# A gated delta-rule scan with a routed expert layer: late slot counts, the first expert's early scatters and later gathers placed elsewhere in a hand-written order

## The chip, the cores and the metric

The kernel runs on one core of one Trainium2 chip. The metric is device microseconds from launch to end, lower is better. A core has engines that run side by side, each through its own queue in program order: PE (matrix products), DVE (elementwise work and reductions), ACT (copies and activation functions), POOL (a general engine, which also issues indirect DMAs) and SP (which here only issues DMAs). A result passes between engines through semaphores, so an instruction that waits holds back everything behind it on its own queue.

## The reference

Two stages. The first is a recurrent attention with a state matrix for each of 4 batches and 8 heads; the second sends every token to one of 8 experts.

```python
B, H, S, D = 4, 8, 768, 48            # attention
N, DM, E, F = 3072, 384, 8, 1024      # experts; N = B * S, DM = H * D
k_n = k / (norm(k) + 1e-6)
for t in range(S):
    y[t] = q[t] @ state
    state = state + beta[t] * outer(k_n[t], v[t] - k_n[t] @ state)
x = y.reshape(N, DM)
logits = x @ w_gate
e = argmax(logits, 1)                 # one expert for each token
out[n] = softmax(logits)[n, e] * (relu(x[n] @ w1[e]) @ w2[e])
```

## The kernel before

**Attention.** The 768 steps are cut into 24 chunks of 32 (`NN = 24`), and the loop `for t in range(NN)` (line 882) runs over them. Inside one chunk the recurrence is solved by small matrix products over all 32 batch-head pairs at once. PE's order in a chunk is written out by hand: `residual` (line 369, product of keys and state into the PSUM bank `kb`, then DVE subtracts it from `v`, line 371), `state_out` (into `yb`), `apply` (line 376, into `kb`, which ACT copies to `u`, line 383), `turn` (line 419, transposes of the row before), `update` (line 385, into the state `S`, which ACT copies to `st` in two halves, line 396), `inside` (line 398, into `yb`), `logits` (line 449, for the chunk before, into `kb`; ACT copies it to `rl`, line 458). The bank `kb` is shared by `residual`, `apply`, `logits` and the counts described below, in different columns.

**Positions.** Between these steps stand seven calls `beside(t, i)` (line 869). Each sets a position `at[0] = 7*t + i` and hands out other work at that place of the order: DVE work from a list of generators up to a budget (`BUD`, 1.4 at i = 0, 1.3, 1.3, 1.3, 0.9, and nothing at i = 5 and 6), then, from chunk 20 on, `count_now()`, then steps of the weight pipeline `W` at the places in `WSL`, then steps of the first expert's early work at the places in `ES`.

**Routing.** `emit_slots` (line 473) is the generator that turns the logits of one to four chunks into a slot in the expert's list: maximum, one-hot `ohb` (lines 488 to 503, DVE); then a `count` on PE (lines 510 to 514, two or more small products into `kb`: how many tokens before this one chose the same expert), copied to `pc` by ACT (line 517); then the position in the list, `sli` (lines 525 to 551, DVE); then a write of the row to DRAM (`xn`, line 554, on SP) and a scatter of the token's number to `st_d` (line 555, on POOL). The count is put on a list `pend`, and `count_now` (line 464) issues everything that is on it. A generator asks for its next part only some positions after the part before (`lag`, 4 for the chunks up to 19, 2 for later ones). After the last chunk a loop (line 942) goes on giving out these steps, one position each, with one step of the early expert work in each of its rounds.

**Weights.** `pieces` (line 586) loads the weights of all experts in pieces of 128 rows (`w1`, 3 pieces of 512 KB) or 256 rows (`w2`, 4 pieces of 384 KB), in the order of experts, through three raw buffers (`load`, line 594, on SP). Each piece is split (line 582) into a rounded part `hi` and the remainder `lo`, so that a product is made of three. For the pieces 0 to 6, those of expert 0, DVE makes both parts; for later ones ACT makes `hi` and DVE `lo`. A piece's split is followed at once by the load of the piece three further on, which needs the same raw buffer. In chunks 20 to 23 the two first loads stand at (20, 3) and (20, 6), and the seven splits at (21, 1), (21, 3), (21, 5), (22, 1), (22, 3), (22, 5), (23, 1).

**Expert 0, early.** When the list of expert 0 has its first 256 tokens (chunks 0 to 15), they are gathered and computed ahead of the expert phase. `early` (line 690) does it in steps: `x` (transposes and splits, 3 steps), `h` (8 steps), `y` (2 steps, each ends with a scatter of 128 rows of the output, line 714). `rest` (line 717) prepares the remaining tokens of expert 0 in two steps, `t` and `o`. `EO` (line 95) is their order: `xxxhhhhhhhhytyo`.

**Expert phase.** For each expert, twelve steps t = 0 to 11 (line 1079): eight of the first product (`h`), then four groups of the second (`y`), each with a scatter of the output. Beside them, `tokens` (line 967) prepares the next expert: at t = 0 `fetch` gathers its rows by four indirect DMAs on POOL (line 632, into one of two buffers `XR`) and `find` loads the list of the one after it; at t = 6 the gate weights; at 8, 9 and 10 the transposes. `run(W)` at the steps in `PC` advances the weights of the next expert.

Of the kernel before, what the change touches and what calls it, by code (L numbers as in the profile page):

```python
# [8 lines left out]
F32 = mybir.dt.float32  # L9
# [4 lines left out]
ALU = mybir.AluOpType  # L14
# [6 lines left out]
NN = S // C  # L21
# [4 lines left out]
DM = H * D  # L26
E = 8
# [6 lines left out]
NG = 3  # L34
GW = [128] * NG + [CAP - 128 * NG]
ROW = DM + E + 2
# [5 lines left out]
def deltanet_moe(ctx, tc, kq, kn_in, v_in, bl_in, w_gate, w1, w2, out):  # L42
    nc = tc.nc
# [31 lines left out]
    W1 = 4  # L75
# [3 lines left out]
    AH = 3  # L79
# [3 lines left out]
    VA = 6  # L83
    RB = {4: 2, 1: 3}
    PL = (1, 3, 5)
    BUD = (1.4, 1.3, 1.3, 1.3, 0.9, 0.0, 0.0)
    TS = 5
    TOK = (0, 6, 8, 9, 10)
# [1 line left out]
    TOK0 = (0, 6, 8, 9, 10)  # L90
    PC0 = (0, 2, 5, 7, 8, 10, 11)
    WSL = ((20, 3), (20, 6), (21, 1), (21, 3), (21, 5), (22, 1), (22, 3), (22, 5), (23, 1))
    ES = ((23, 1), (23, 3), (23, 4), (23, 6))
    EF = tuple(range(0, 16))
    EO = 'xxxhhhhhhhhytyo'
# [2 lines left out]
    rp = ctx.enter_context(tc.tile_pool(name="rp", bufs=1, side="left"))  # L98
# [138 lines left out]
    at = [-1000]  # L237
# [91 lines left out]
    def lane_ops(tb):  # L329
        T = tiles[tb]  # L330
        lg, lw = T["lg"], T["lw"]
        G = nc.gpsimd if tb in PL else nc.vector
        for c in range(31):
# [128 lines left out]
    pend, order_ = [], []  # L462

    def count_now(more=lambda: None):
        now = list(pend)
        for x in now:
            x[0]()
        more()
        for x in now:
            x[1]()  # L470
            pend.remove(x)

    def emit_slots(n0, w, row, rl):
# [43 lines left out]
            nc.scalar.copy(out=pc, in_=pp)  # L517
            when.append(at[0])

        pend.append((count, keep))  # L520
        yield 0.2
        while not when or order_[0] != n0:
            yield None
# [45 lines left out]
    def run(gen, steps=1):  # L569

        for _ in range(steps):
            if next(gen, tiles) is tiles:
                return False
        return True
# [4 lines left out]

    KD, KF = DM // 128, FF // 128  # L580

    def split(hi, lo, src, copy=nc.scalar.copy):
        copy(out=hi, in_=src)  # L583
        nc.vector.tensor_tensor(out=lo, in0=src, in1=hi.bitcast(F32), op=ALU.subtract)  # L584

    def pieces():

        todo = []
        for e in range(E):
            for nm, src, kk, ff, st in (("w1", w1[e], KD, FF, 1), ("w2", w2[e], KF, DM, 2)):  # L590
                todo += [(e, nm, src.rearrange("(k p) f -> p k f", p=128), kk, ff, st, j) for j in range(0, kk, st)]
        raws = []

        def load(k):
            e, nm, sv, kk, ff, st, j = todo[k]
            raw = wq[0].tile([128, FF], F32, name=f"{nm}r{e}_{j}", tag="wr", bufs=3)
            if 0 < k < AH:
                nc.scalar.copy(out=raw[0:1, 0:1], in_=ident[0:1, 0:1])
            raws.append(raw[:, 0:st * ff].rearrange("p (k f) -> p k f", k=st))
            nc.sync.dma_start(out=raws[k], in_=sv[:, j:j + st])  # L600

        for k in range(AH):
            load(k)
            yield
        for k, (e, nm, sv, kk, ff, st, j) in enumerate(todo):
            if j == 0:
                WW[e][nm] = [wq[e % 2].tile([128, kk, ff], F32R, name=f"{nm}{x}{e}", tag=f"{nm}{x}") for x in "hl"]
            hi, lo = WW[e][nm]
            split(hi[:, j:j + st], lo[:, j:j + st], raws[k], nc.vector.tensor_copy if k < 7 else nc.scalar.copy)
            if k + AH < len(todo):  # L610
                load(k + AH)
            yield

    WW = [{} for _ in range(E)]

# [16 lines left out]
    def fetch(e, g0=0, g1=NG + 1, nt=NN):  # L632
        for g in range(g0, g1):
            nc.gpsimd.indirect_dma_start(out=XR[e][:, g], out_offset=None, in_=xn[0:128 * nt],  # L634
                                         in_offset=bass.IndirectOffsetOnAxis(ap=XI[e][:, g, 0:1], axis=0),
                                         bounds_check=128 * nt - 1, oob_is_err=False)

    def smalls(e, g0, g1, pool):

        n = g1 - g0  # L640
        ex = pool.tile([128, n, E], F32, name=f"ex{e}_{g0}", tag=f"ex{n}", bufs=2)
        gt = pool.tile([128, n], F32, name=f"gt{e}_{g0}", tag=f"gt{n}", bufs=2)
        x = XR[e][:, g0:g1]
        nc.scalar.activation(out=ex, in_=x[:, :, DM:DM + E], func=AF.Exp)
        nc.vector.tensor_reduce(out=gt, in_=ex, axis=AX.X, op=ALU.add)
        nc.vector.tensor_scalar(out=gt, in0=gt, scalar1=1e-9, scalar2=None, op0=ALU.add)
        nc.vector.reciprocal(gt, gt)
        return gt, XI[e][:, g0:g1, 1:2]
# [37 lines left out]
    def scatter(yo, idx):  # L686
        nc.gpsimd.indirect_dma_start(out=out, out_offset=bass.IndirectOffsetOnAxis(ap=idx, axis=0), in_=yo,  # L687
                                     in_offset=None, bounds_check=N - 1, oob_is_err=False)

    def early():  # L690

        w = 128 * G0
        xe = er_[0].tile([128, 2 * KD, w], F32R, name="xe")
        x = [xe[:, i * KD:i * KD + KD] for i in range(2)]
        for d in range(KD):
            pt = psg_[-1].tile([128, w], F32, name=f"xt{d}", tag="g")
            for g in range(G0):
                nc.tensor.transpose(pt[:, g * 128:g * 128 + 128], XR[0][:, g, d * 128:(d + 1) * 128], ident)
            split(x[0][:, d], x[1][:, d], pt)
            yield  # L700
        he = er_[0].tile([128, KF, 2, w], F32R, name="he")
        hs = [(he[:, f, 0], he[:, f, 1]) for f in range(KF)]
        for f in range(KF):
            ps = psg_[-1].tile([128, w], F32, name=f"h0_{f}", tag="g")
            first(ps, WW[0]["w1"], x, slice(f * 128, f * 128 + 128))
            relu(*hs[f], ps)
            yield
        gt, idx = smalls(0, 0, G0, er_[0])
        for g in range(G0):
            ps = psg_[-1].tile([128, DM], F32, name=f"y0_{g}", tag="g")  # L710
            second(ps, lambda f: [h[:, g * 128:g * 128 + 128] for h in hs[f]], WW[0]["w2"])
            yo = er_[0].tile([128, DM], F32, name=f"yo0_{g}")
            nc.scalar.activation(out=yo, in_=ps, func=AF.Copy, scale=gt[:, g:g + 1])
            scatter(yo, idx[:, g])
            yield

    def rest():
# [20 lines left out]
    er_ = []  # L738
# [70 lines left out]
    W = None  # L809
# [55 lines left out]
    def ahead_step():  # L865
        if order and not (order[0] == "o" and len(last) < DEF):
            run(other if order.pop(0) in "to" else ahead)

    def beside(t, i):
# [5 lines left out]
        if t >= NN - 4:  # L875
            count_now()
        for _ in range(WSL.count((t, i))):
            run(W)
# [3 lines left out]
    for t in range(NN):  # L882
        if t % TB == 0 and t > 0:
            finish_lane(t // TB)
            if t == NN - TB:
# [5 lines left out]
                W = pieces()  # L891
                run(W)
        g = t + GA
# [44 lines left out]
    i = 0  # L938
# [3 lines left out]
    while fine:  # L942
        at[0] += 1
        for x in list(fine):
            for _ in range(4):
                if next(x, -1) == -1:
                    fine.remove(x)
                    break
        count_now()
        if i in EF:  # L950
            ahead_step()
        i += 1
    while order:
        ahead_step()
# [12 lines left out]
    def tokens(e, X):  # L967
        if e == 0:
            X.extend(X0["x"])
            find(0, NG)  # L970
            find(1)
            yield
        fetch(e, 0 if e > 0 else NG)
        if 0 < e < E - 1:
            find(e + 1)
        yield
        xr = XR[e]
        g0 = 0 if e > 0 else G0
        X.append(smalls(e, g0, NG + 1, xp_))
        if e == 0:  # L980
            return
        xh = xp_.tile([128, KD, CAP], F32R, name=f"xh{e}", tag="xh", bufs=2)
        xl = xp_.tile([128, KD, CAP], F32R, name=f"xl{e}", tag="xl", bufs=2)
        w = CAP - NG * 128
        X[0:0] = [xh, xl]
        yield
        for d in range(KD):
            pt = px.tile([128, CAP], F32, name=f"xt{e}_{d}", tag="xt")
            for g in range(NG):
                nc.tensor.transpose(pt[:, g * 128:g * 128 + 128], xr[:, g, d * 128:(d + 1) * 128], ident)  # L990
            nc.tensor.transpose(pt[:, NG * 128:], xr[0:w, NG, d * 128:(d + 1) * 128], ident[0:w, 0:w])
            split(xh[:, d], xl[:, d], pt)
            yield
# [82 lines left out]
    for e in range(E):  # L1076
        tok = tokens(e + 1, XX[e + 1]) if e + 1 < E else iter(())
        main = ffn(e, WW[e], XX[e])
        for t in range(KF + NG + 1):
            if (e, t) == (E - 1, 1):  # L1080
                beyond()
                nc.gpsimd.drain()
            if e == 0 and t in (0, TS):
                run(tok0)
            if t in (TOK if e > 0 else TOK0):
                run(tok)
            run(main)
            if t in (PC if e > 0 else PC0):
                run(W)
# [3 lines left out]
    op = ctx.enter_context(tc.tile_pool(name="op", bufs=1))  # L1093
# [23 lines left out]
    if True:  # L1117
# [62 lines left out]
        yo = small("oyo", (128, DM))  # L1180
# [47 lines left out]
```

## Time and profile before

| | |
|---|---|
| median of 3 runs | 520.28 us (511.73 to 525.62) |
| the profiled execution | 519.29 us |
| its span, first to last instruction | 517.1 us |
| mean granted clock of PE | 0.962 |
| attention and routing, up to the first row of the expert phase | 0 to 284.5 us |
| expert phase and end | 284.5 to 517.1 us |

A row of the timeline gives the start, the duration of one or several merged instructions, engine, line, operation, tiles, and in square brackets the idle time before it with what ended that. A row of windows gives, for one stretch of time, the busy time and number of instructions of each engine, the mean clock that was granted to PE (1.00 is full speed), the busy share of the DMA engines and the bytes they moved. A row of waits gives who waited for whom, the total, the number of times and the longest. Where several semaphores are waited for, the profile names the one that came last by its own records; the name can be wrong.

### The profile page before, as it was taken

The numbers are of one execution on the slowest core, as the hardware profiler recorded it, in microseconds if no ns is written. First come the engines' busy times: TensorE is split into PE (matmuls) and PEld (weight loads), VectorE is DVE, ScalarE is ACT, GpSimd is POOL, SyncE is SP. The second block draws the span as 40 slices with busy tenths as digits, with TensorE's granted clock in tenths as the row PEclk, the third lists the DMA queues.
The fourth block names the chain that finished last, engine by engine and source line by source line (L and its number), as shares of the span: only waits on it lengthen the run. The fifth ranks groups of instructions, "written<-read, shape, count | busy, mean of one in ns | idle before, by whom it ended". The sixth has DMA issues, their size and how long they took to land. (4 is left out here: it accounts for less than half of the span.)

```text
span 517.1 us, 18086 instructions
## 1 busy us (share of the span) xinstructions
PE 461.0 (89%) x7694; PEld 420.4 (81%) x7694; DVE 301.9 (58%) x739; ACT 247.6 (48%) x594; POOL 225.1 (44%) x337
## 2 busy tenths in 40 slices
PE   5688979979987887787979999999999999999995
PEld 4576868767866666677869899999999999999995
DVE  1899599995997941447332765372553636264330
ACT  1326656655756666555222555453544544354230
POOL 8038880488953888441133440322514231241202
PEclk9999999998988999987589999999999999999999
DMA  5891334362422453458410555463454556352101
GB/s 153 244 231 41 112 101 137 98 173 83 109 60 51 120 100 85 74 151 217 126 46 17 153 179 173 123 200 111 122 174 140 165 147 184 101 173 81 36 3 45
DMA packets 35629, 62.53 MB, mean 121 GB/s; under 512 B 8951, under 2 KB 26567, under 8 KB 35536
## 3 DMA queue, kind: packets, MB, share of 16 engines
q1 hardware_dynamic: 30608, 51.42, 37.1%
q0 software_dynamic: 4928, 9.75, 6.0%
q8 instruction: 72, 1.18, 1.0%
q14 instruction: 21, 0.17, 0.1%
HBM read 53.20 MB, written 10.40 MB: 123 GB/s over the span
## 5 line engine op out<-in xcount | busy, mean ns | idle before, releaser
L687 POOL DMA_INDIRECT out_dram<-yo,xi x32 | 32.7, 1023 | 161.9 <-ACT yo L1024 100.1
L684 PE MATMUL y<-w2h,hx 128*128 128x384 f32 x352 | 93.4, 339 | 0.0
L584 DVE TENSOR_TENSOR w2l<-w2r,w2h 128x768 fp32r<-128x768 f32 x32 | 30.6, 960 | 68.2 <-ACT w2h L583 67.6
L684 PEld LDWEIGHTS y<-w2h,hx 128*128 128x128 f32 x352 | 63.8, 188 | 0.9
L658 PE MATMUL h<-xh,w1h 128*128 128x384 f32 (+1 forms) x168 | 62.2, 370 | 0.0
L684 PE MATMUL y<-w2l,hx 128*128 128x384 f32 x176 | 59.0, 335 | 0.0
L658 PE MATMUL h<-xl,w1h 128*128 128x384 f32 (+1 forms) x168 | 57.7, 343 | 0.0
L658 PE MATMUL h<-xh,w1l 128*128 128x384 f32 (+1 forms) x168 | 57.6, 343 | 0.0
L340 POOL TENSOR_TENSOR lw<-lw,tmp 128x31 f32<-128x31 f32 (+15 forms) x93 | 53.7, 578 | 7.3
L337 POOL TENSOR_TENSOR tmp<-lg,lw 128x31 f32<-128x31 f32 (+15 forms) x93 | 50.6, 544 | 6.7
L677 ACT ACTIVATE hx<-h 128x448 fp32r<-128x448 f32 (+1 forms) x64 | 33.0, 518 | 39.4 <-PE h L658 33.7
L357 ACT ACTIVATE v<-v,nt_all 128x48 f32<-128x48 f32 x192 | 48.3, 327 | 3.4 <-DVE nt_all L286 3.2
L678 DVE SCALAR_TENSOR_TENSOR hx<-h,hx 128x448 fp32r<-128x448 f32 (+1 forms) x64 | 37.4, 586 | 19.0 <-ACT hx L677 14.6
L1024 ACT ACTIVATE yo<-y,gt 128x384 f32<-128x384 f32 (+1 forms) x22 | 12.6, 575 | 70.7 <-PE y L684 51.1
L555 POOL DMA_INDIRECT st_d<-idi,sli x24 | 25.4, 1060 | 47.1 <-DMA st_d<-idi,sli 28.9
L396 ACT COPY st<-S 48x768 f32<-48x768 f32 x46 | 36.5, 793 | 19.7 <-PE S L390 17.9
L634 POOL DMA_INDIRECT xr<-xn,xi x33 | 38.0, 1151 | 14.9 <-issue 7.5
L371 DVE TENSOR_TENSOR v<-v,kb 128x384 f32<-128x384 f32 x23 | 12.6, 548 | 44.6 <-PE kb L362 31.3
L684 PEld LDWEIGHTS y<-w2l,hx 128*128 128x128 f32 x176 | 33.1, 188 | 0.0
L584 DVE TENSOR_TENSOR w1l<-w1r,w1h 128x1024 fp32r<-128x1024 f32 x24 | 29.4, 1225 | 5.9 <-ACT w1h L583 5.1
L383 ACT COPY u<-kb 128x384 f32<-128x384 f32 x24 | 11.5, 479 | 43.6 <-PE kb L381 30.2
L658 PEld LDWEIGHTS h<-xl,w1h 128*128 128x128 f32 x168 | 31.7, 189 | 0.4
(193 smaller groups left out, 1019.7 us busy)
## 6 DMA issues: line engine op xcount, KB each, us to landing
w1r<-in_moe_w_dram SPq DMA_DIRECT2D x24, 512.0 KB
w2r<-in_moe_w_dram SPq DMA_DIRECT2D x32, 384.0 KB
kq<-in_kq_dram SPq DMA_DIRECT2D x16, 448.0 KB
kn<-in_k_dram SPq DMA_DIRECT2D x24, 224.0 KB
xn<-row SPq DMA_DIRECT2D x24, 197.0 KB
v<-in_v_dram SPq DMA_DIRECT2D x24, 192.0 KB
kq<-in_kq_dram SPq DMA_DIRECT2D x16, 224.0 KB
xr<-xn,xi POOLq DMA_INDIRECT x33, 3.8
```

Of the source, the lines that this page charges most:

```text
L337: G.tensor_tensor(out=x, in0=lg[:, w:32, c:c + 1].broadcast_to([128, m, w]), in1=lw[:, c:c + 1, 0:w].broadcast_to([128, m, w]), op=ALU.mult)
L340: G.tensor_tensor(out=lw[:, w:32, 0:w], in0=lw[:, w:32, 0:w], in1=x, op=ALU.subtract)
L357: nc.scalar.activation(out=vn[:, h], in_=vn[:, h], func=AF.Copy, scale=nt[:, h:h + 1])
L396: nc.scalar.copy(out=st_t[r, :, :, c], in_=sv[r, :, :, c])
L555: nc.gpsimd.indirect_dma_start(out=st_d, out_offset=bass.IndirectOffsetOnAxis(ap=sli[:, j:j + 1], axis=0), in_=idi[:, n0 + j], in_offset=N ...
L584: nc.vector.tensor_tensor(out=lo, in0=src, in1=hi.bitcast(F32), op=ALU.subtract)
L634: nc.gpsimd.indirect_dma_start(out=XR[e][:, g], out_offset=None, in_=xn[0:128 * nt], in_offset=bass.IndirectOffsetOnAxis(ap=XI[e][:, g, 0: ...
L658: nc.tensor.matmul(ps[:, 0:c] if c else ps, lhsT=w[:, d, fs], rhs=x_[:, d, 0:c] if c else x_[:, d], start=(n == 0), stop=(n == len(terms) ...
L677: nc.scalar.activation(out=hh, in_=ps, func=AF.Relu)
L678: nc.vector.scalar_tensor_tensor(out=hl, in0=ps, scalar=0.0, in1=hh.bitcast(F32), op0=ALU.max, op1=ALU.subtract)
L684: nc.tensor.matmul(ps, lhsT=h(f)[h_], rhs=w2[w][:, f, :], start=(n == 0), stop=(n == len(terms) - 1))
L687: nc.gpsimd.indirect_dma_start(out=out, out_offset=bass.IndirectOffsetOnAxis(ap=idx, axis=0), in_=yo, in_offset=None, bounds_check=N - 1, ...
```

## The change

There are five edits.

1. `count_now`: from chunk 20 on (position 140 and later) a count is issued only when the position is at least two (`CL = 2`) past the one where it was put on the list. Before, it was issued at the end of the same position.
2. `split` takes the engine of the remainder as an argument, and for pieces 0 to 6 the remainder is made by POOL; DVE still makes the rounded part.
3. The loads of pieces 7, 8 and 9 (the first of expert 1) no longer follow the splits of pieces 4, 5 and 6; they are three steps of their own, given out in rounds 2, 4 and 6 of the loop after the last chunk (`WF`).
4. `early`: the two output tiles of the `y` steps lie in a buffer of the rows' ring instead of the pool that is closed before the expert phase, and their scatters are kept on a list `held` and issued at step 2 of expert 0.
5. `tokens`: the gathers of experts 2 to 7 leave step 0 of the expert before; the gather of expert e + 2 is issued at step 6 (`FT`) of expert e, six steps earlier.

```diff
+    FT = 6
+    CL = 2
+    WF = (2, 4, 6)
...
     def count_now(more=lambda: None):
-        now = list(pend)
+        now = [x for x in pend if at[0] < 7 * (NN - W1) or at[0] >= x[2] + CL]
...
-        pend.append((count, keep))
+        pend.append((count, keep, at[0]))
...
-    def split(hi, lo, src, copy=nc.scalar.copy):
+    def split(hi, lo, src, copy=nc.scalar.copy, rest=nc.vector):
         copy(out=hi, in_=src)
-        nc.vector.tensor_tensor(out=lo, in0=src, in1=hi.bitcast(F32), op=ALU.subtract)
+        rest.tensor_tensor(out=lo, in0=src, in1=hi.bitcast(F32), op=ALU.subtract)
...
-            split(hi[:, j:j + st], lo[:, j:j + st], raws[k], nc.vector.tensor_copy if k < 7 else nc.scalar.copy)
-            if k + AH < len(todo):
+            split(hi[:, j:j + st], lo[:, j:j + st], raws[k], *((nc.vector.tensor_copy, nc.gpsimd) if k < 7 else (nc.scalar.copy, nc.vector)))
+            if k + AH < len(todo) and not 4 <= k < 7:
                 load(k + AH)
             yield
+            for j in range(7, 7 + AH) if k == 6 else ():
+                load(j)
+                yield
...
+    held = []
...
+        ye = rp.tile([128, 4, ROW], F32, name="ye", tag="row4", bufs=RB[4])
         for g in range(G0):
...
-            yo = er_[0].tile([128, DM], F32, name=f"yo0_{g}")
+            yo = ye[:, g, 0:DM]
             nc.scalar.activation(out=yo, in_=ps, func=AF.Copy, scale=gt[:, g:g + 1])
-            scatter(yo, idx[:, g])
+            held.append((yo, idx[:, g]))
...
         if i in EF:
             ahead_step()
+        if i in WF:
+            run(W)
         i += 1
...
-        fetch(e, 0 if e > 0 else NG)
+        if e < 2:
+            fetch(e, 0 if e > 0 else NG)
...
+            if (e, t) == (0, 2):
+                for x in held:
+                    scatter(*x)
+            if t == FT and e + 2 < E:
+                fetch(e + 2)
             if t in (TOK if e > 0 else TOK0):
                 run(tok)
```

## The prediction

> **What bounds the kernel now.** I read the page first, then windows cut at the stages, then PE's waits, then the timeline of chunks 20 to 23 and of the loop behind them, because that is where the edits lie.
>
> ```profile
> span 517.1 us, 18086 instructions
> PE 461.0 (89%) x7694; PEld 420.4 (81%) x7694; DVE 301.9 (58%) x739; ACT 247.6 (48%) x594; POOL 225.1 (44%) x337
> PEclk9999999998988999987589999999999999999999
> ```
> ```profile
> 230.00:238.40 8.40, 6.05 (x209) 5.17 (x206) 6.00 (x18) 5.17 (x18) 2.53 (x2) 1.00 0.93 270
> 238.40:258.90 20.50, 19.60 (x276) 17.51 (x276) 9.02 (x30) 5.90 (x16) 3.96 (x4) 0.51 0.53 138
> 258.90:269.00 10.10, 6.91 (x44) 6.12 (x43) 3.46 (x18) 2.48 (x10) 4.79 (x6) 0.81 0.25 59
> 269.00:284.50 15.50, 15.16 (x103) 14.56 (x101) 4.34 (x20) 4.57 (x9) 3.96 (x4) 1.00 0.07 14
> 284.50:517.00 232.50, 225.57 (x1313) 218.11 (x1312) 112.49 (x191) 102.10 (x173) 64.18 (x62) 1.00 0.43 128
> ```
>
> The expert phase, from 284.5 us on, is PE at work without a break: 225.6 of 232.5 us, and what is missing is mostly the end, where outputs land. No edit removes PE work, so time can come only from before 284.5 us. There PE has holes, and a stretch of 20.5 us at half clock (0.51), in which 19.6 us of PE work is done that would take about half as long at full clock.
>
> The holes that the edits touch are those in front of the late counts:
>
> ```profile
> PE kb L511 <- DVE ohb L503: 3.1, 3, 1.6
> PE kb L511 <- DVE w2l L584: 1.9, 1, 1.9
> PE kb L511 <- DVE w1h L583: 0.9, 1, 0.9
> PE kb L381 <- ACT pc L517: 0.5, 2, 0.3
> PE h L658 <- DVE hx L678: 0.5, 1, 0.5
> PE h L658 <- ACT xb L583: 0.4, 1, 0.4
> ```
>
> The first four rows are of 205 to 280 us, and sum to 6.4 us. The last two are all that PE waits for between 284.9 and 511 us: 0.9 us. The fourth is of use for its mechanism: `apply` writes columns of `kb` that the count doesn't use, and still waits until ACT has read the count. So any two uses of `kb` exclude each other.
>
> **Edit 1, counts two positions later: gain of 6.4 us, and a new wait.** In the chunks the count leaves the place between `state_out` and `apply` (or behind `apply`) and goes behind `update` (chunk 20) or behind `inside` (21 to 23); in the loop it goes two rounds later, behind two more `h` groups, when its `ohb` has long been made.
>
> ```profile
> 262.92 0.19 PE L511 MATMUL kb<-ohb,ltri 128*128 128x8 bf16 x1 [1.01 <-DVE ohb L503]
> 268.34 0.18 PE L511 MATMUL kb<-ohb,ltri 128*128 128x8 bf16 x1 [1.56 <-DVE ohb L503]
> ```
>
> These two of the loop go: 2.6 of the 6.4 us. In the chunks the same count now meets something else. Chunk 21 before:
>
> ```profile
> 230.38 1.04 PE L390 MATMUL S<-u,kn 32*112 32x96 f32 x32
> 231.88 1.61 ACT L396 COPY st<-S 48x768 f32<-48x768 f32 x2 [1.14 <-PE S L390]
> 232.41 0.83 PE L456 MATMUL kb<-wg,xT 128*128 128x8 f32 x6
> 233.54 0.17 ACT L458 COPY rl<-kb 128x8 f32<-128x8 f32 x1
> 233.76 0.87 PE L362 MATMUL kb<-st,kq 112*32 112x96 f32 x32 [0.51 <-ACT rl L458]
> ```
>
> `logits` (L456) runs beside the state copies, so that only the copy `rl` (0.17) lies between them and the next `residual` (L362). With the count in front of it, ACT's order is: state copies, `pc`, `rl`. `logits` writes `kb` and must wait for `pc`: copies to 233.49, `pc` to about 233.7, `logits` to 234.5, `rl` to 234.8, `residual` at 234.8 instead of 233.76. That is 1.05 us in each of chunks 20, 21 and 22, **+3.1 us**. In chunk 23 there is no state copy; I take nothing. Bounds: 0, if the exclusion didn't hold for these columns, and 3.1. I take the upper one, since the row on `apply` shows that it holds. What waits for the delayed `pc` is the slot chain, two positions or more later; its end is the gather for step `t`:
>
> ```profile
> 266.51 1.02 POOL L634 DMA_INDIRECT xr<-xn,xi  x1 [0.31 <-issue]
> 277.18 0.49 PE L723 MATMUL xt<-ident,xr 128*128 128x128 f32 x3
> ```
>
> From issue to use are 10.7 us. PE loses some 4 us ahead of it (the two holes and the clock), and the gather is issued in round 3 instead of round 0; that uses the slack up and leaves no wait that I can name. Zero, at worst 2 us.
>
> **Edit 2, remainders on POOL: where the new cost is.** DVE loses seven operations, none of which ended a wait of PE by itself (the row that names `w2l` is taken up below); gain zero. POOL gets them:
>
> ```profile
> L279 POOL TENSOR_TENSOR lg<-lg,lw x3: 1961/2035/3239, 33.5 to 164.4; 128x1024 f32<-128x1024 f32 x3
> 200.33 0.61 POOL L340 TENSOR_TENSOR lw<-lw,tmp 128x220 f32<-128x220 f32 x1
> 200.35 0.63 DVE L492 TENSOR_TENSOR row<-rl,mx 128x16 f32<-128x16 f32 x1
> 217.26 0.18 DVE L492 TENSOR_TENSOR row<-rl,mx 128x16 f32<-128x16 f32 x1
> ```
>
> A remainder of a `w1` piece costs 2.0 us there, of a `w2` piece about 1.5 (an estimate: three quarters of the elements). And a DVE operation with two inputs in SBUF that meets one on POOL stands until it ends: L492 took 0.63 us beside POOL's 0.61, and 0.18 alone. The slot chain consists of such operations; each of POOL's seven can hold it for up to 2 us.
>
> The Trainium skill (SBUF — State Buffer, section "SBUF: two separate sides") says that DVE and POOL share one port pair as an exclusive lock, held for a whole instruction. The two L492 rows agree with it. By it the seven remainders could hold DVE for up to 12 us in all; the sum here goes by the queue below.
>
> What counts more is POOL's queue. The remainder is the last reader of a raw buffer, and it stands behind scatters that wait for the landing of the scatter before:
>
> ```profile
> 224.18 0.33 SPq L600 DMA_DIRECT2D w1r<-in_moe_w_dram  x1
> 228.91 0.69 DVE L583 CAST w1h<-w1r 128x1024 fp32r<-128x1024 f32 x1
> 229.02 0.38 SPq L600 DMA_DIRECT2D w2r<-in_moe_w_dram  x1
> 232.04 1.03 POOL L555 DMA_INDIRECT st_d<-idi,sli  x1 [0.30 <-issue]
> 238.84 0.99 POOL L555 DMA_INDIRECT st_d<-idi,sli  x1 [5.77 <-DMA st_d<-idi,sli]
> 246.39 0.55 DVE L371 TENSOR_TENSOR v<-v,kb 128x384 f32<-128x384 f32 x1 [3.35 <-PE kb L362]
> 248.65 1.42 PE L381 MATMUL kb<-v,wt 32*32 32x48 f32 x52 [0.26 <-ACT pc L517]
> ```
>
> The order on POOL is: scatter of chunk 16 (ends 233.1), piece 0 (to 235.1), scatter of 17, pieces 1 and 2, scatter of 18, and so on. If the scatter lands early, because the load that went out at 229.02 now goes out only at 235, scatter 17 ends at 236.2, piece 2 at 240.3; if it lands as before, scatter 17 ends at 239.8, piece 2 at 243.9. Then the load of piece 5 goes out, and is there 4.7 us later (224.18 to 228.91): 245.0 or 248.6. DVE's rounded part of piece 5 stands at (22, 5), in front of L371 of chunk 23, which `apply` waits for: 0.55 each, so `apply` at 246.1 or 249.7. With the other terms `residual` of chunk 23 would be at about 242.8 and `apply` at 244.9. So this costs 1.2 to 4.8 us. I take **+2.0**, nearer to the early end, since the DMA queues are emptier where loads go out later.
>
> **Edit 3, three loads later.** They take 1.5 MB out of 241 to 250 us and put it into the loop, where the window of 258.9 shows 59 GB/s. Their splits begin with expert 0, behind 284.5. Zero; if SP were held, piece 7 would be late there, bounded by one landing, 4.7 us.
>
> **Edits 4 and 5, scatters and gathers.**
>
> ```profile
> 284.81 1.05 POOL L634 DMA_INDIRECT xr<-xn,xi  x1 [0.50 <-issue]
> ```
>
> That gather stood behind an early scatter that waited for `yo`; it can now go a few us sooner. But PE's waits in the expert phase are 0.9 us in all, so that is the upper bound for both edits; the lower is POOL's two scatters, 2 us, off PE's path. I take zero.
>
> **The clock.** The stretch of half clock begins after a hole of PE:
>
> ```profile
> 236.12 0.17 DVE L503 TENSOR_TENSOR ohb<-oh,m_all 128x8 bf16<-128x8 f32 x1
> 238.44 0.18 PE L511 MATMUL kb<-ohb,ltri 128*128 128x8 bf16 x1 [1.88 <-DVE w2l L584]
> 244.76 1.50 PE L362 MATMUL kb<-st,kq 112*32 112x96 f32 x32 [0.26 <-ACT rl L458]
> ```
>
> The same 32 products took 0.87 us at 233.76 and 1.50 at 244.76. At most 19.6 x (1 - 0.51) = 9.6 us can be had back, at least nothing. The removed 1.88 us hole is the largest ahead of the drop, but chunk 23 has little PE work between its waits, and it gets a new wait by edit 2. I take a third, **-3.2 us**, and for the loop, where dense products follow one another without the two holes, 6.91 x (1 - 0.81) = **-1.3 us**.
>
> The Trainium skill (TensorE: Matmul & The Clock Gate, section "Part 1: The HAM clock gate") lets the clock fall after an idle window of about 3.4 us. The trace does not agree: the longest hole here is under 2.2 us, and the clock fell. By that rule no hole here would cost clock, both terms would be zero, and the sum 518.0.
>
> **The sum.** -6.4 + 3.1 + 2.0 - 3.2 - 1.3 = -5.8 us, against the profiled execution of 519.3 us (span 517.1 and 2.2 around it): **513.5 us**. The median of the runs shown, 520.28, is 1.0 above that execution; the runs spread from 511.73 to 525.62, so that about 2% is what a measurement of this kernel can tell from no change.
>
> **Rivals.**
> - *The clock stays up.* If chunk 23 keeps its windows dense, most of the 9.6 us comes back, say 7.5: -6.4 + 3.1 + 2.0 - 7.5 - 1.3 = -10.1, 509.2 us. For it: the drop follows one hole. Against it: PE was almost fully busy through the stretch (19.60 of 20.50) and the clock did not recover, so small products alone don't lift it.
> - *POOL's queue holds chunk 23: slower.* If scatter 17 waits as before, L371 is 4.8 us late; one remainder in the way of the slot chain adds 2.0, and the clock gains nothing: -6.4 + 3.1 + 4.8 + 2.0 = +3.5, 522.8 us. It decides from where DVE's L371 of chunk 23 comes later than about 248. For it: the 5.77 us wait on POOL. Against it: fewer loads at that time.
> - *The stall at 238.44 is not the count's.* Its `ohb` was ready at 236.29, and the named `w2l` is none of its inputs. If PE stands there whatever comes next, 1.9 us of the gain and the 3.2 of the clock are gone: -6.4 + 1.9 + 3.1 + 2.0 - 1.3 = -0.7, 518.6 us.
>
> **Chances.** Forecast 0.44, clock stays up 0.22, POOL's queue 0.17, stall stays 0.17. The forecast's own range is 510.5 to 517. The range of 8 in 10 reaches beyond 509.2 and 522.8 by the spread of a run: 506.5 to 524. Faster by over 2% means below 508.9: half of the clock's rival and some of the forecast's lower end, 0.18. Slower by over 2% means above 529.7, further than any case with a price: 0.04. Within 2%: 0.78.
>
> **What will show it.** In the changed profile: no row of L511 with more than 0.3 us in front (edit 1); PE's `logits` (L456) waiting for ACT `pc` in chunks 20 to 22, about 0.6 us each; POOL's remainder rows at 1.5 to 2.0 us, and the SP loads of pieces 3 to 6 later than 229 to 238; L371 of chunk 23 near 245 to 246; the half-clock stretch shorter than 20 us; the expert phase as long as before. I am wrong if L456 doesn't wait, if DVE stands in front of L371 for over 4 us, or if the last `residual` comes with the clock at full speed.

## The result and the profile after

The changed kernel takes 521.84 us (median of 20 runs, 518.13 to 527.27), the kernel before beside it 518.41 us (20 runs, 511.73 to 527.45). The ratio is **1.0117 [1.009, 1.0143]**: 1.2% slower, about 6 us. The ratio leaves out every run more than 1.5% above the fastest of its kernel, nine of the 20 of before and one of the changed kernel's, and so shows a larger loss than the medians (3.4 us). The time lies in the forecast range, but the forecast was a gain of 5.8 us; the sign is wrong.

The page of the changed kernel, span, busy times and the clock in 40 slices:

```profile
span 522.5 us, 18092 instructions
PE 464.4 (89%) x7694; PEld 423.2 (81%) x7694; DVE 307.4 (59%) x732; ACT 247.5 (47%) x594; POOL 240.5 (46%) x344
PEclk9999987997999999978699899999999999999998
```

DVE has seven instructions fewer and is busy 5.5 us longer. To see where, the trace is cut at two marks that every version has: the first product of `residual` of chunk 19, and the first product of the expert phase. Between them lies **the stretch** (A in some expectations), behind it the expert phase (B), whose first part is expert 0. Windows of the kernel before, stretch and expert 0, then those of the changed kernel (columns: length, busy time and instructions of PE, PEld, DVE, ACT, POOL, clock of PE, DMA share, GB/s):

```profile
206.70:284.90 78.20, 65.66 (x1181) 58.58 (x1181) 32.84 (x119) 31.21 (x95) 24.30 (x33) 0.83 0.41 105
284.90:303.40 18.50, 17.96 (x126) 16.77 (x126) 11.05 (x26) 8.84 (x19) 6.18 (x6) 1.00 0.52 148
```

```profile
209.70:282.80 73.10, 62.84 (x1181) 55.82 (x1181) 37.91 (x113) 30.96 (x95) 36.81 (x39) 0.86 0.43 110
282.80:308.10 25.30, 21.23 (x126) 19.58 (x126) 10.92 (x26) 8.84 (x19) 15.51 (x12) 0.87 0.46 134
```

In these two executions the stretch got 5.1 us shorter, and expert 0 got 6.8 us longer with the same 126 products. Together that is 1.7 of the 5.4 us between the two spans; 3.0 us more lie ahead of the first mark (209.7 against 206.7), where no edit acts. That the 5.1 is near the forecast gain is chance: against a second profile of before, shown further down (72.8 and 19.4 us), the stretch is 0.3 us longer and expert 0 5.9. PE's waits of the changed kernel from the stretch to the end of expert 0 say why:

```profile
PE xt L1002 <- DMA xr<-xn,xi: 3.9, 2, 2.2
PE kb L514 <- DVE ohb L506: 2.4, 1, 2.4
PE kb L516 <- issue: 1.6, 1, 1.6
PE kb L459 <- ACT pc L520: 1.0, 2, 0.8
PE kb L384 <- DVE v L374: 0.4, 1, 0.4
```

(Lines moved: L514, L506, L520, L459, L374, L384, L587 are L511, L503, L517, L456, L371, L381, L584 of before.) The holes of the loop are gone; one wait for `ohb` is new, and the transposes of expert 1 (L1002) stand for its gather. Two stretches of the changed kernel's timeline show the two mechanisms. First DVE beside POOL (rows between are left out):

```profile
237.55 2.37 POOL L587 TENSOR_TENSOR w1l<-w1r,w1h 128x1024 fp32r<-128x1024 f32 x1
238.20 1.77 DVE L529 TENSOR_TENSOR pos<-base,pc 128x16 f32<-128x16 f32 x1
240.24 1.01 POOL L558 DMA_INDIRECT st_d<-idi,sli  x1 [0.31 <-DVE row L495]
240.37 0.17 DVE L542 SCALAR_TENSOR_TENSOR pos<-ovr,pos 128x16 f32<-128x16 f32 x1
240.57 5.40 DVE L544 TENSOR_TENSOR pos<-pos,ohb 128x16 f32<-128x16 f32 x1
241.26 4.67 POOL L587 TENSOR_TENSOR w1l<-w1r,w1h 128x1024 fp32r<-128x1024 f32 x2
245.90 0.15 DVE L506 TENSOR_TENSOR ohb<-oh,m_all 128x8 bf16<-128x8 f32 x1
246.11 0.17 PE L514 MATMUL kb<-ohb,ltri 128*128 128x8 bf16 x1 [2.37 <-DVE ohb L506]
247.68 3.02 DVE L586 CAST w2h<-w2r 128x768 fp32r<-128x768 f32 x2 [0.84 <-DMA w2r<-in_moe_w_dram]
251.08 1.31 DVE L529 TENSOR_TENSOR pos<-base,pc 128x8 f32<-128x8 f32 x1
252.85 2.55 DVE L542 SCALAR_TENSOR_TENSOR pos<-ovr,pos 128x8 f32<-128x8 f32 x1
```

The step on `pos` at 240.57 works on 16 columns; its neighbour takes 0.17 us, it takes 5.40, until both of POOL's remainders have ended at 245.93. Behind it on DVE's queue stands the `ohb` that the count on PE needs. Six rows are held: two steps of 16 columns, two of 8, a pair of copies of 0.55 us each, and a step of 1.10 us at 261.34 that isn't shown. The excess is 1.60 + 5.23 + 1.14 + 2.38 + 1.92 + 0.93 = 13.2 us. The lock that the Trainium skill describes (SBUF — State Buffer, section "SBUF: two separate sides") agrees, also in that a one-input copy is held; the 12 us that the prediction worked out from it and left out of the sum are near the 13.2 that DVE lost. Three of the six begin 0.3 to 0.7 us ahead of the remainder's own row, while POOL's scatter in front of it is on record (240.24). The scatter alone holds nothing: in the kernel before, 12 of DVE's short two-input steps between 205 and 290 us begin beside one, and none takes over 0.17 us.

Second, the end of the slot chain, with three rows of the kernel before and then the changed kernel (rows between are left out):

```profile
279.38 1.15 SPq L628 DMA_DIRECT2D xi<-st_d  x2
290.27 1.00 POOL L634 DMA_INDIRECT xr<-xn,xi  x1 [0.30 <-issue]
294.20 0.49 PE L990 MATMUL xt<-ident,xr 128*128 128x128 f32 x3
```

```profile
275.16 1.02 POOL L558 DMA_INDIRECT st_d<-idi,sli  x1 [0.30 <-issue]
279.68 1.00 POOL L558 DMA_INDIRECT st_d<-idi,sli  x1 [3.50 <-DMA st_d<-idi,sli]
282.81 1.15 SPq L634 DMA_DIRECT2D xi<-st_d  x2
286.23 1.65 POOL L640 DMA_INDIRECT xr<-xn,xi  x1 [5.56 <-DMA xi<-st_d]
293.49 1.00 POOL L640 DMA_INDIRECT xr<-xn,xi  x1 [0.30 <-issue]
293.76 0.72 PE L1002 MATMUL xt<-ident,xr 128*128 128x128 f32 x2 [2.21 <-DMA xr<-xn,xi]
296.19 0.47 PE L1002 MATMUL xt<-ident,xr 128*128 128x128 f32 x1 [1.72 <-DMA xr<-xn,xi]
```

Each scatter to `st_d` waits until the one before has landed. With the counts two rounds later the last one goes out at 279.68, 3.1 us before the expert phase; the lists are read at its start (before: at 279.38, 5.6 us ahead of it). The five gathers, the last four of which are expert 1's, begin 3.4 us behind the start of the expert phase and end at 294.49; before, they began 0.1 us ahead of it (284.81) and ended at 291.27, and the transposes at 294.20 found them landed.

### The profile page after: what moved, and what is told of

Same layout as the page of the kernel before. It is cut to its first block, busy times and chain, and to the rows that moved or that the text cites. A ratio compares the mean times of both kernels' runs of the same rounds, so it can differ in the third digit from the quotient of the medians.

```text
span 522.5 us, 18092 instructions
## 1 busy us (share of the span) xinstructions
PE 464.4 (89%) x7694; PEld 423.2 (81%) x7694; DVE 307.4 (59%) x732; ACT 247.5 (47%) x594; POOL 240.5 (46%) x344
## 5 line engine op out<-in xcount | busy, mean ns | idle before, releaser
L690 PE MATMUL y<-w2h,hx 128*128 128x384 f32 x352 | 95.3, 345 | 0.0
L693 POOL DMA_INDIRECT out_dram<-yo,xi x30 | 30.9, 1029 | 123.0 <-ACT yo L1036 65.0
L587 DVE TENSOR_TENSOR w2l<-w2r,w2h 128x768 fp32r<-128x768 f32 x28 | 26.9, 962 | 74.6 <-ACT w2h L586 74.5
L690 PEld LDWEIGHTS y<-w2h,hx 128*128 128x128 f32 x352 | 65.6, 193 | 0.9
L690 PE MATMUL y<-w2l,hx 128*128 128x384 f32 x176 | 60.1, 342 | 0.0
L684 DVE SCALAR_TENSOR_TENSOR hx<-h,hx 128x448 fp32r<-128x448 f32 (+1 forms) x64 | 37.2, 586 | 18.9 <-ACT hx L683 17.4
L374 DVE TENSOR_TENSOR v<-v,kb 128x384 f32<-128x384 f32 x23 | 12.7, 550 | 46.6 <-PE kb L365 31.4
L406 PE MATMUL yb<-u,gq 64*64 64x48 f32 x768 | 29.3, 228 | 3.3 <-issue 3.3
```

What stands on the lines that cost most here:

```text
L406: nc.tensor.matmul(yb[r, D * h:D * h + D], lhsT=gq[r, h], rhs=u[r, h], start=(n == 0 and h == 0), stop=True, tile_position=(64 * c, 64 * c ...
L587: rest.tensor_tensor(out=lo, in0=src, in1=hi.bitcast(F32), op=ALU.subtract)
L684: nc.vector.scalar_tensor_tensor(out=hl, in0=ps, scalar=0.0, in1=hh.bitcast(F32), op0=ALU.max, op1=ALU.subtract)
L690: nc.tensor.matmul(ps, lhsT=h(f)[h_], rhs=w2[w][:, f, :], start=(n == 0), stop=(n == len(terms) - 1))
```

## The experiments

Two theories were set against each other: POOL's remainders hold DVE and so the slot chain (edit 2), and the late counts make expert 1's gather late (edit 1). All ratios are to the kernel before, run on the same chip. "Idle" is the stretch less PE's busy time; busy time goes with the clock, idle time less so. Stretch, idle time, clock and expert 0 are those of one profiled execution, the ratio that of many; the profiled execution of e7, 524.15 us, lies well above that kernel's median of 519.86.

| kernel | remainders | ratio | stretch | PE busy | idle | clock | expert 0 |
|---|---|---|---|---|---|---|---|
| before | DVE | 1 | 78.2 | 65.7 | 12.5 | 0.83 | 18.5 |
| before, again (e11) | DVE | 1.0034 [0.9993, 1.0075] | 72.8 | 58.6 | 14.2 | 0.93 | 19.4 |
| edit 1 alone (e2) | DVE | 0.9983 [0.9941, 1.0025] | 69.8 | 62.6 | 7.2 | 0.85 | 21.1 |
| edits 3 to 5 (e8) | DVE | 0.9994 [0.995, 1.0038] | 77.5 | 65.6 | 11.9 | 0.82 | 19.3 |
| all but edit 2 (e3) | DVE | 1.0003 [0.9957, 1.005] | 68.5 | 60.1 | 8.4 | 0.90 | 25.1 |
| e3, loop's counts at once, 4 lists (e6) | DVE | 0.9991 [0.9948, 1.0033] | 76.3 | 64.0 | 12.3 | 0.87 | 19.4 |
| e3, transposes later, 4 lists (e9) | DVE | 0.9972 [0.9922, 1.0022] | 68.0 | 59.1 | 8.9 | 0.92 | 17.8 |
| the same, again (e12) | DVE | 0.9943 [0.9895, 0.9992] | 70.2 | 61.5 | 8.7 | 0.88 | 21.5 |
| edit 2 alone (e7) | POOL | 1.0072 [1.0037, 1.0106] | 78.5 | 65.3 | 13.2 | 0.83 | 19.3 |
| POOL's work beside DVE's (e10) | POOL | 1.0131 [1.0083, 1.0178] | 76.2 | 59.4 | 16.8 | 0.89 | 18.9 |
| all but edit 1 (e1) | POOL | 1.0167 [1.0088, 1.0245] | 87.8 | 71.7 | 16.1 | 0.73 | 18.6 |
| all, loop's counts at once (e4) | POOL | 1.0152 [1.0113, 1.019] | 75.4 | 61.6 | 13.8 | 0.89 | 19.1 |
| e4, 4 lists (e5) | POOL | 1.0066 [1.0015, 1.0116] | 77.6 | 65.2 | 12.4 | 0.82 | 18.7 |
| changed | POOL | 1.0117 [1.009, 1.0143] | 73.1 | 62.8 | 10.3 | 0.86 | 25.3 |

**All but edit 1.**

```diff
-    CL = 2
+    CL = 0
```

> The changed kernel with edit 1 alone undone: late counts are issued at once again. Stretch A is the time from the residual of chunk 19 to the first product of the expert phase (78.3 us before, 73.1 changed), stretch B from there to PE's last product (226.1 before, 232.8 changed). Theory G (the two later rounds of the loop make the lists of expert 0 and 1 late, and expert 1's gather with them): PE's waits for the gather (3.9 us) are gone, B is back at 226 to 227, A rises by 3 to 5 us, since the holes at the counts are back; total within 0.5% of the kernel before. Rival P (POOL's queue, filled by the remainders, makes the gather late): the gather still ends waits of 2 us or more, B stays at 230 or more, total 1% or more above the kernel before. Rival C (only the clock differs from run to run): B varies without any wait for the gather.

Ratio 1.0167 [1.0088, 1.0245], no better than the whole change (the intervals overlap). The theory of the late lists had put it within 0.5% of the kernel before. PE's waits in the stretch and expert 0:

```profile
PE kb L514 <- DVE ohb L506: 9.8, 4, 4.0
PE xt L1003 <- DMA xr<-xn,xi: 0.8, 1, 0.8
```

The gather is nearly in time again and expert 0 takes 18.6 us: without edit 1 its 6.8 us are gone. But the counts, issued at once, stand for `ohb` again, 9.8 us in all. Of these 4.0 us lie beside POOL's remainders; 3.3 us lie in chunk 20, ahead of the first remainder (228.04), where the second profile of before has 3.1 us too, and 2.6 us are the two holes of the loop. That the late counts hide part of what edit 2 costs fits 4.0 us here against 2.4 in the changed kernel, but the ratios don't show it.

**Edit 1 alone.**

```diff
+    CL = 2
-        now = list(pend)
+        now = [x for x in pend if at[0] < 7 * (NN - W1) or at[0] >= x[2] + CL]
-        pend.append((count, keep))
+        pend.append((count, keep, at[0]))
```

> The kernel before with edit 1 alone added. Theory G: the late counts alone make expert 1's gather late. Here the gather also stands behind the two early scatters on POOL, so PE waits for it at least as long as in the changed kernel (4 us or more), B is 230 or more, A is 3 to 5 us shorter than 78.3; total 0.5 to 1.5% slower than before. Rival P: without the remainders on POOL the gather is in time, B is 226 to 227, and the total is 0.5 to 1% faster than before.

PE idles 7.2 us in the stretch instead of 12.5, expert 0 takes 2.6 us more, 1.4 of them a wait for the gather, and expert 5, which waits 1.9 us for a gather too, 2.3 us more. So edit 1 alone brings 2.6 of the 6.8 us; the rest comes only with edits 3 to 5 beside it, and the runs don't show why. Ratio 0.9983 [0.9941, 1.0025]: no difference that can be told, where both theories expected one.

**All but edit 2.**

```diff
-*((nc.vector.tensor_copy, nc.gpsimd) if k < 7 else (nc.scalar.copy, nc.vector))
+*((nc.vector.tensor_copy, nc.vector) if k < 7 else (nc.scalar.copy, nc.vector))
```

> The changed kernel with edit 2 alone undone: DVE makes the remainders of pieces 0 to 6 again. Theory G: PE still waits 2 us or more for expert 1's gather, B 230 or more; the weights of expert 0 go out earlier, so the wait in front of the count of chunk 22 (2.4 us) shrinks below 1 and A is 1 to 2 us shorter than 73.1; total 0 to 0.5% faster than the changed kernel. Rival P: the waits for the gather go, B 226 to 228, total 1% faster than the changed kernel.

One word takes the loss back: 1.0003 [0.9957, 1.005]. PE's waits:

```profile
PE xt L1002 <- DMA xr<-xn,xi: 3.9, 2, 2.3
PE kb L384 <- DVE v L374: 2.1, 1, 2.1
PE xt L732 <- DMA xr<-xn,xi: 1.7, 1, 1.7
PE kb L459 <- ACT pc L520: 1.5, 2, 0.8
```

No wait for `ohb` is left; the wait of expert 1 for its gather is there without POOL's remainders. New waits stand where the counts were: `apply` for `v`, step `t` for its gather, `logits` for `pc`, 5.3 us together. They take back part of what the removed holes gave.

**All, the loop's counts at once.**

```diff
-at[0] >= x[2] + CL]
+at[0] >= x[2] + CL or at[0] > 7 * NN - 1]
```

> The changed kernel, with counts held two positions only inside chunks 20 to 23 and issued at once in the loop behind them (the counts of chunks 22 and 23). Theory G: the last two lists are two rounds (about 2 to 3 us) earlier; the holes of 1.0 and 1.6 us in the loop are back, so A is 2 to 3 us longer than 73.1, and the wait for the gather shrinks by as much or goes: B 226 to 229; total 0.3 to 1% faster than the changed kernel. Rival P: no change of B.

Expert 0 is back at 19.1 us, but the ratio stays at 1.0152 [1.0113, 1.019] instead of falling by 0.3 to 1%: expert 1 takes 33.6 us instead of 28.4. SP's wait, then the timeline:

```profile
SPq L631 <- DMA out_dram<-yo,xi: 21.3, 5, 8.5
```

```profile
312.51 5.77 SPq L603 DMA_DIRECT2D w2r<-in_moe_w_dram  x4
316.07 0.83 ACT L586 CAST w2h<-w2r 128x768 fp32r<-128x768 f32 x1 [5.40 <-DMA w2r<-in_moe_w_dram]
317.39 0.45 PE L690 MATMUL y<-w2h,hx 128*128 128x384 f32 x1 [1.26 <-ACT hx L683]
```

The lists `xi` have three buffers. Expert 3's list takes that of expert 0 and waits for expert 0's last out-scatter. In this run the held scatters and expert 2's gathers stand ahead of that on POOL; SP waits, the weight piece behind it on SP's queue comes late, and ACT, standing for the piece, keeps the `hx` that PE needs. In the changed kernel SP has the same wait (22.1 us, 5.1 at the longest), and PE doesn't stand for it. So edits 4 and 5 can have a price where another delay comes to theirs.

**The same, with a fourth list buffer; and that with the remainders on DVE.**

```diff
-tag="xi", bufs=3)
+tag="xi", bufs=4)
```

> The run with the loop's counts at once (changed kernel otherwise), with a fourth buffer for the slot lists `xi`. In that run SyncE's load of expert 3's list stood for the out-scatters of expert 0, whose buffer it takes (SPq L631, up to 8.5 us), and the piece of w2 behind it came late: ACT waited 5.40 us for it, PE 1.26 and 0.46 us for hx, and the clock fell to half for 6.8 us; expert 1 took 33.6 us. Theory (list buffer): SyncE no longer waits there, expert 1 takes 28.4 us, the ratio to before falls by 0.010 to about 1.005. Rival (chance): the waits of expert 1 belonged to that one execution, or the loads are late for another reason; then expert 1 stays at 33 us, or the ratio stays at 1.015 +- 0.003 although expert 1 is short.

> As the run beside it, and the seven remainders on VectorE again. Theory: the two costs found add up. Without POOL's remainders the chunks take 68 to 71 us from the residual of chunk 19 to the expert phase (before: 78.3), expert 0 takes 19 us, expert 1 28.4 us, and the ratio to before is 0.985 to 0.990. Rival: counts put off in the chunks alone are worth less than they look, the clock or a new wait takes it back, and the ratio is 0.995 to 1.000, as with the counts' delay alone on the kernel before (0.998).

With four buffers SP's wait is gone, expert 1 takes 28.4 us and the ratio falls to 1.0066 [1.0015, 1.0116], as the list theory had it. With the remainders on DVE it is 0.9991 [0.9948, 1.0033]: the forecast of 0.985 to 0.990 missed. Its loop has the two holes again (`ohb`, 3.0 us), `apply` of chunk 22 stands 3.1 us for nothing that the profile names (see the last section), and idle time is 12.3 us, as before. Counts put off in the chunks alone gain nothing that can be told.

**Edit 2 alone, and edits 3 to 5 alone** (the latter is the changed kernel with `CL = 0` and the remainders on DVE).

> The kernel before with the seven remainders on POOL as its only edit. Theory (POOL's remainders hold VectorE's two-input steps): the stretch from the residual of chunk 19 to the expert phase grows from 78.3 to about 87 us, PE waits for `ohb` several times (before: 3.1 us in all), expert 0 stays at 18.4 to 19 us, ratio 1.012 to 1.018. Rival (the prediction's size, 2 us, all by POOL's queue): about 80 us, ratio 1.003 to 1.006.

> The changed kernel without the counts' delay and with the remainders on VectorE: what is left of the change is the three later loads, the held out-scatters and the early gathers. If these cost nothing by themselves, as the prediction has it: stretch 78 us, expert 0 18.5 us, expert 1 28.4 us, ratio 1.000 +- 0.003. Rival: with expert 0 in time again, the held scatters and the gathers of expert 2 stand ahead of expert 0's out-scatters on POOL, expert 3's list waits for these, the weight pieces behind it on SyncE come late, and expert 1 takes 31 to 34 us: ratio 1.005 to 1.010.

Edit 2 alone is slower, 1.0072 [1.0037, 1.0106], by half of what was expected, and its stretch is 78.5 us instead of the 87 expected, no longer than the first one of before. Edits 3 to 5 alone make no difference (0.9994 [0.995, 1.0038]); expert 0 takes 19.3 us and expert 1 28.4, so by themselves the held scatters and early gathers don't reach PE.

**POOL's work without the late buffers.** DVE keeps its remainders, so the raw buffers come free as before, and POOL subtracts zero from each remainder in place:

```diff
+            if k < 7:
+                l3 = lo[:, j:j + st]
+                nc.gpsimd.tensor_tensor(out=l3, in0=l3.bitcast(F32), in1=zz[:, 0:st].unsqueeze(2).broadcast_to([128, st, ff]), op=ALU.subtract)
```

> The kernel before; VectorE keeps its seven remainders and so frees the raw buffers as before, and POOL runs seven operations of the same sizes beside them (it takes zero from each remainder in place, out of a small tile of zeros read over and over). Theory (VectorE is held while POOL runs, or POOL's queue delays the scatters): PE waits for `ohb` 7 us or more in the stretch, ratio 1.005 to 1.010, as with the remainders moved to POOL (1.0072). Rival (the prediction's: late raw buffers, late loads): no more than before, 3.1 us for `ohb` and ratio 1.000 +- 0.003.

1.0131 [1.0083, 1.0178], above the 1.005 to 1.010 expected. Its window of the stretch and its timeline:

```profile
205.70:281.90 76.20, 59.40 (x1182) 52.68 (x1182) 42.50 (x120) 31.25 (x95) 37.22 (x41) 0.89 0.38 109
```

```profile
231.70 2.54 DVE L526 TENSOR_TENSOR pos<-base,pc 128x16 f32<-128x16 f32 x1
232.29 1.91 POOL L615 TENSOR_TENSOR w1l<-w1l,zz 128x1024 fp32r<-128x1024 f32 x1
235.17 0.18 PE L511 MATMUL kb<-ohb,ltri 128*128 128x8 bf16 x1 [2.46 <-DVE ohb L503]
237.32 4.51 DVE L539 SCALAR_TENSOR_TENSOR pos<-ovr,pos 128x8 f32<-128x8 f32 x1
238.04 3.76 POOL L615 TENSOR_TENSOR w1l<-w1l,zz 128x1024 fp32r<-128x1024 f32 x2
249.87 0.17 PE L511 MATMUL kb<-ohb,ltri 128*128 128x8 bf16 x1 [5.65 <-DVE ohb L503]
```

DVE has the work of before and is busy 42.5 us instead of 32.8. PE waits 11.2 us in front of the counts, where the two profiles of before have 5.9 and 8.1. Late raw buffers are not needed for the loss; DVE being held is enough. POOL's scatters stand behind the added work too, but PE waits for no gather in this stretch. Nor is a lower clock needed: PE is busy 59.4 us, near the 58.6 of the second profile of before.

**The gather covered.** As all but edit 2, with four lists, and

```diff
-    TOK0 = (0, 6, 8, 9, 10)
+    TOK0 = (0, 8, 9, 10, 11)
```

> Counts two rounds later everywhere, the seven remainders on VectorE, a fourth list buffer, and the gate weights and transposes of expert 1 later inside expert 0 (steps 8 to 11 in place of 6 to 10), so that the products of a y group stand between the late gather and its first use. Theory (the gain of the counts' delay is real, and expert 0's wait for the gather gives it back): stretch 68 to 70 us, expert 0 19.5 to 21 us instead of 25.1, ratio 0.988 to 0.993. Rival (the shorter stretch of the profiled runs is not that of most runs, or the wait only moves): ratio 0.997 to 1.003, or expert 0 still at 24 us or more.

Expert 0 falls to 17.8 us (expert 1 takes 1.0 us more), and the profiled execution is the shortest of all, span 507.5 us; but the ratio is 0.9972 [0.9922, 1.0022], not the 0.988 to 0.993 expected. Was one execution flattering it, or had the first profile of before been a bad one? Both were run again:

> The kernel before once more, unchanged, for a second profile of it: how far does the stretch from the residual of chunk 19 to the expert phase (78.3 us in the first profile) vary from one execution to the next? Theory (the stretch is set by its waits, and the counts' delay shortens it): 75 to 80 us again. Rival (the stretch goes with the clock of the one execution, and the profile of before was a slow one): 73 us or less. Ratio 1.000 +- 0.004 either way.

> The version with the counts' delay, remainders on VectorE and expert 1's transposes later, once more and beside the run of the kernel before: stretch 66 to 71 us again (first profile 68.0) and ratio 0.988 to 0.995 by the theory that its gain is real; 74 us or more, or ratio 0.997 to 1.003, by the rival that the one profile flattered it.

The windows and one row of the kernel before, in its second profile:

```profile
236.90:249.40 12.50, 9.89 (x264) 8.62 (x264) 9.12 (x30) 4.66 (x13) 1.45 (x2) 1.00 0.88 244
205.50:278.30 72.80, 58.56 (x1181) 52.25 (x1181) 32.80 (x120) 31.08 (x95) 26.16 (x35) 0.93 0.42 112
```

```profile
236.99 0.18 PE L511 MATMUL kb<-ohb,ltri 128*128 128x8 bf16 x1 [1.93 <-DVE w2h L583]
```

The unchanged kernel's stretch is 72.8 us here and 78.2 in its first profile: 7.1 us less of PE busy time, at a clock of 0.93 instead of 0.83, and 1.7 us more idle time. PE's hole in front of the same count is 1.93 us (1.88 in the first), and no half clock follows it: 1.00 for the next 12.5 us, where the first profile had 0.51 for 20.5 us. The better version gives 0.9943 [0.9895, 0.9992] the second time; its expert 0 takes 21.5 us there, with 1.9 us of waits for the gather, so the gather is covered in one of its two profiles only. It is the fastest of this study, by 0.3 and 0.6%, while the kernel before against itself came out at 1.0034, so that differences of 0.3% are not told by these ratios; a gain of 2% is not in it.

## Why the prediction was wrong

Four pairs differ only in the engine of the remainders: changed less e3, e1 less e8, e5 less e6, e7 less before. They give 0.0114, 0.0173, 0.0075 and 0.0072, each larger than its uncertainty (0.003 to 0.009); the mean is 0.011, 5.6 us of 515. The pair at the changed kernel itself gives 5.9 us. Late transposes (e9, e12 against e3) give 0.3 and 0.6%, 2.3 us in the mean. The counts' delay with late transposes (e9, e12 against e8) is worth 0.4%, -1.9 us. The uncertainty of each of these two, 0.006, is larger than the difference itself.

5.9 + 2.3 - 1.9 = 6.3, against 6.0 measured. This agreement proves little: the three differences are one chain from edits 3 to 5 alone to the changed kernel, so they must add up to 1.0117 less 0.9994. It says where the prediction missed: edit 2 is 5.9 instead of 2.0, expert 1's gather 2.3 instead of 0, and edit 1 with the clock -1.9 instead of -3.3 - 4.5 = -7.8. These misses, 3.9, 2.3 and 5.9, make up the 12 us between forecast and result.

- **Edit 2, +2.0: mis-sized, and what makes the changed kernel slower.** Without it the time is that of before (1.0003): the forecast gain was lost elsewhere, the loss is here. The prediction named the hold, "each of POOL's seven can hold it for up to 2 us", with the rows for it, and then went on with "What counts more is POOL's queue" and "the sum here goes by the queue below". The hold was given no term in the sum. It measured 13.2 us of DVE's time and 5.9 us of the kernel's. The loads of pieces 3 to 6 did go out late (239.95 to 249.80 instead of 229 on), but PE waited 0.4 us in all for `v`, and the run with the buffers free in time lost as much. POOL's remainders took 2.37 and 1.83 us, not 2.0 and 1.5.
- **The clock, -3.2 and -1.3: wrong.** Both terms were read from one execution. The same kernel, run again, has the hole and not the slow stretch behind it. In all four pairs PE is busy longer in the stretch with the remainders on POOL (2.7, 6.1, 1.2 us, and 3.2 against the mean of the two profiles of before, but -0.4 against the first), while idle time grows by less than 2 us in three of them. That a lower clock carries the rest of edit 2's cost is not shown by this: two profiles of one kernel differ by 7.1 us, and POOL's work beside DVE's loses 1.3% without it. How 13.2 us of DVE's time become 5.9 of the kernel's stays open.
- **Edit 1's slot chain, "uses the slack up and leaves no wait that I can name": wrong.** The step named the gather for `t` and overlooked the one behind it: expert 1's. PE waits 3.9 us there and the products after it run at a lower clock (0.87 in expert 0); with edits 3 to 5 beside it that is 6.8 us in the profile. In time it is worth 1.6 to 3.1 us by the runs with later transposes.
- **Edit 1, -6.4 + 3.1 = -3.3: right in direction on the spot, too large in the time.** One of the four rows of the 6.4, the 1.9 us at 238.44, was not the count's (see the rivals). PE's idle time in the stretch with DVE's remainders is 12.5, 14.2, 11.9 without the delay and 7.2, 8.4, 8.9, 8.7 with it: -4.6 us in the mean of single profiles. `logits` waits for `pc` as forecast, 0.8 us at the longest, 1.0 us in all (forecast about 0.6 each, three times). But the time falls by 1.9 us only; 1.0 us comes back in expert 1, whose transposes were put off, and the rest isn't accounted for.
- **Edits 3, 4, 5, zero: right by themselves** (0.9994 [0.995, 1.0038]). The bound "PE's waits in the expert phase are 0.9 us in all, so that is the upper bound" was unsound all the same: waits seen before bound what can be gained, not what can be lost, and e4 lost 5.2 us in expert 1 to the lists.
- **The rivals.** "POOL's queue holds chunk 23" had the direction and nearly the time (522.8), by a mechanism that fell: L374 of chunk 23 came at 250.62, 40.9 us behind the mark, against 39.7 before. The 2.0 us it allowed for the slot chain were the part that was real, and too little. "The stall at 238.44 is not the count's" holds as far as the hole goes: with the delay and DVE's remainders no count stands there, and e2, e12 and e6 still have a hole of 1.09, 1.19 and 3.08 us, in front of the last product of `apply`; only e3 and e9 have none. The last section shows what stands before it. The time of this rival, 518.6, is within 0.2% of no change. "The clock stays up" was true of the second profile of before, without any edit.

## What to carry to other kernels

Work moved to POOL wasn't off DVE here: while POOL's remainders ran, DVE's short steps with two SBUF inputs stood. So count the length of each POOL operation against every DVE chain that lies beside it. When a step is put off, follow its result through all its readers to the last one, and ask how much work covers each; waits that are there now say nothing of waits to come. A hole in front of an instruction need not be that instruction's: move the instruction and see whether the hole goes with it. A slow clock in one profile is no term for a sum: profile the unchanged kernel twice before you price it.

## What the runs showed of the hardware

A DVE step of 0.17 us took 5.40, over two POOL operations back to back: DVE didn't get in between them.

The clock fell without a large hole, too: with edit 1 alone, this window holds no hole on PE over 1.1 us, and PE ran at half speed for all 17.1 us:

```profile
234.00:251.10 17.10, 15.49 (x312) 13.18 (x302) 9.40 (x35) 5.06 (x16) 3.43 (x4) 0.50 0.72 197
```

The second profile of before has a hole of 1.93 us and full clock behind it. So holes of this size don't decide the clock by themselves; what does, these runs don't settle.

A hole can come from outside the order of the program. These rows are of chunk 22 in edit 1 alone, in e12 and in e6, one row of each:

```profile
237.46 0.23 PE L382 MATMUL kb<-v,wt 32*32 32x48 f32 x1 [1.09 <-issue]
239.54 0.20 PE L384 MATMUL kb<-v,wt 32*32 32x48 f32 x1 [1.19 <-issue]
242.41 0.20 PE L384 MATMUL kb<-v,wt 32*32 32x48 f32 x1 [3.08 <-issue]
```

Of the 64 products of `apply` the last one stands, for nothing that the profile names. In the trace's records of DMA packets, one of 16 KB on the queue of kind `instruction` lands 1.58, 1.56 and 1.75 us before these holes end. The holes of about 2 us in front of the count of chunk 22 are alike: the packet lands 1.52 us before the end in the kernel before (238.44), 1.61 in its second profile (236.99) and 1.58 with edits 3 to 5 alone (238.90). Over the 14 profiles, from 20 to 505 us, 56 of PE's holes are longer than 0.7 us and put down to `issue`, and all end 1.2 to 1.8 us behind such a packet; a moment picked at random lies there in 8% of cases. So PE most likely stood there for instructions still to come. No run changes these packets, so that is not shown, and what an instruction packet's lateness depends on stays open.
